# Expert weights loaded in pieces during attention, one key tile less on VectorE: a pre-LN attention and MLP kernel on one Trainium2 core

## The chip, the cores and the metric

The kernel runs on one core of a Trainium2 chip. A core has five engines with a queue of their own each, which keep only to the order of their own queue: TensorE (PE in the profile, its weight loads PEld), VectorE (DVE), ScalarE (ACT), GpSimd (POOL) and SyncE (SP, which here issues nearly all transfers). They wait for each other by semaphores. The metric is the device time of the whole program in microseconds.

## The reference

Attention with one shared key and value head, then an MLP for the eight best-scored rows, both behind a layer norm. S = 2048 rows, D = 448, 16 heads of 28, F = 1792.

```python
x = A_x
h = x + _A_ref(_layernorm(x), A_wq, A_wk, A_wv, A_wo)
    # q: 16 heads of 28; k, v: one head; softmax(q k^T * 28**-0.5) v, heads joined, @ wo
h2 = h + _B_ref(_layernorm(h), B_w_r, B_w_gate, B_w_up, B_w_down)
    # x: the normed rows; r = x @ w_r; the 8 rows with the largest r:
    # y = ((silu(x_sel @ w_gate) * (x_sel @ w_up)) @ w_down) * sigmoid(r_sel)
    # result: x, with y added to its 8 rows
```

## The kernel before, in words

**Blocks and key tiles.** The queries are cut into 16 blocks of 128 rows, the keys into 16 tiles of 128. One key tile of one block is four *strips* of scores, 128 keys by 512 columns (four heads by 128 queries), each made by one matmul `ps<-Q,K` (L815). A tile goes one of two ways.

- **ACT tile** (`act_tile`, `spill`): two strips at a time lie in two PSUM banks, and one ScalarE instruction takes the exponential of both (`P<-ps`, L870, 128x1024). A tile is two of these *units*. Four matmuls `ps<-P,Vs` (L845) add its product with V to the block's sum in bank 7.
- **DVE tile** (`dve_tile`): VectorE clips each strip into a 16-bit integer whose bits, read as bf16, are a rough exponential (`Y<-ps`, L891, four per tile). GpSimd adds two constants to a copy of the tile (`Yc<-Y`, L902, two per tile), and TensorE multiplies all three versions with three scaled copies of V: twelve matmuls of L845 where an ACT tile has four.

`_ND` gives for each block how many of its 16 tiles go the DVE way: 87 of 256 before. V has a column of ones, so the block's sum also holds the softmax denominators.

**The head.** x arrives in six loads. For each of seven groups of tiles (0; 1; 2 and 3; 4 and 5; 6 and 7; 8 to 11; 12 to 15) `group` computes the statistics, normalizes (`of`, L738), transposes on TensorE (L749), copies out (`xnT`, L754) and projects K (L621, `ps<-xnT,wk_rep`) and V. VectorE writes K's first copy (L764). The second copy, for the other two strips of a tile, is made by two DMAs `K<-K` on SP's queue, and the scores of the tile wait for them. `q_project` makes Q of a block. `weights` issues the output projection `wo` in four DMAs, each of which waits for the one before it, and the MLP's gate and up weights: `wg_sb` and `wu_sb`, each one DMA of 1344 KB and one of 224 KB.

**Between blocks.** When a block's products are done, `evict` copies bank 7 (`Ot`, L929). The denominators then go out to DRAM and back in another layout (`l_scr<-Ot`, `Lall<-l_scr`), VectorE takes reciprocals (`Rc`, L935), and these go out and come back broadcast (`l_scr<-Rc`, `Rb<-l_scr`). `On` (L938) multiplies them in. `out_proj` adds x and multiplies with `wo`, and VectorE and ScalarE make the row's second norm (`of`, L988), which is stored in `n_rows` and in the output. All these transfers stand in SP's queue, in order, and an instruction that waits there holds up those behind it.

**The end.** `stage1` loads the down weights in one DMA of 1568 KB (`wd_sb`, which lies over `xnT`) and preselects eight rows out of each of the first 14 blocks: their addresses go out (`cidx<-gidx`) and GpSimd gathers them (`wqx<-n_rows,cidx`, L1066). `tail` finishes the last block, selects the best eight rows and runs the MLP on them.

**What sets the order.** The functions record operations with a duration, reads and writes. `_Flow.plan` then lays them out once, at build time, from those durations and a table of weights (`_W`, `_WIN`, `_LOOK`, `_LATE`, `_HOLD`) and fixes each engine's order. Nothing is reordered on the chip. Bank 7 holds the running sum; the other seven banks are handed out by the plan.

Of the kernel before, what the change touches and what calls it, by code (L numbers as in the profile page):

```python
# [506 lines left out]
def _fast(nc, G, sb, ps, psb, flag, scr, rows, A_x, A_wq, A_wk, A_wv, A_wo, B_w_r, B_w_gate, B_w_up, B_w_down, out):  # L507
    S, D, H = A_x.shape[1], A_x.shape[2], 16
    DH = D // H
    FF = B_w_gate.shape[1]  # L510
# [416 lines left out]
    def evict(b):  # L927
# [10 lines left out]
        G.op(DV, lambda e: e.tensor_tensor(On[:, rb, :, :].rearrange("p h n -> p (h n)"), Ot[:, rb, :], Rb[:, rb, :],  # L938
                                           ALU.mult), 599, reads=[("Ot", rb), ("Rb", rb)], writes=[("On", rb)], lock=True)

# [860 lines left out]
```

## Time and profile before

| | before |
|---|---|
| median of 3 runs | 364.43 us (364.39 to 366.26) |
| the profiled execution | 365.21 us, span 363.2 us |
| ScalarE busy | 327.8 us (90%), 407 instructions |
| TensorE matmuls busy | 327.5 us (90%) |
| VectorE busy | 318.0 us (88%), 663 instructions |
| GpSimd busy | 194.3 us (54%) |
| mean granted TensorE clock | 0.968 |
| DMA traffic | 16.36 MB, mean 45 GB/s |

Busy shares are averages over stages. Three stages have different limits: the head (to about 45 us), in which keys are made and ScalarE often has no scores to work on, the long middle, and the tail after the last exponential. In the timeline a row gives start, duration, engine and line, operation, tile and count; idle time before it and what ended it stand in brackets. "SPq" rows are the issuing of a DMA, not its transfer.

### The profile page before, as it was taken

The page shows a single profiled execution, that of the slowest core. Times are in us where ns is not written, and L with a number is a line of the kernel's source. Part 1 is how long each engine was busy: PE and PEld are TensorE (multiplying, and loading weights), DVE is VectorE, ACT ScalarE, POOL GpSimd, SP SyncE. Part 2 cuts the span into 40 slices and gives each one's busy share as a digit, 9 for nine tenths or more (in the row PEclk, how much of TensorE's full clock was granted, in tenths as well). Part 3 has the DMA queues.
Part 4 walks back from the last instruction along what each step waited for, and adds up shares of the span by engine and source line. Part 5 has one row for each costly group of instructions (what it writes and reads, how often), then busy time and mean ns, then how long its engine had stood idle before and what let it go on. Part 6 is the DMA issues. An engine that isn't in the chain of part 4 may idle for free.

```text
span 363.2 us, 8869 instructions
## 1 busy us (share of the span) xinstructions
PE 327.5 (90%) x3690; PEld 109.8 (30%) x3690; DVE 318.0 (88%) x663; ACT 327.8 (90%) x407; POOL 194.3 (54%) x206
## 2 busy tenths in 40 slices
PE   3955989999999999999999999999999999999984
PEld 2623323232323222223232222323232322222344
DVE  7854669998989989999998999999988999999783
ACT  5543799999999999999999999999999999999950
POOL 8010027874656565866564656658563758675501
PEclk9976899999999999999999999999999999999995
DMA  7563000001001100101010101010011240010110
GB/s 181 130 230 137 10 7 3 15 20 28 32 19 41 31 27 29 32 5 56 4 47 14 55 3 43 19 30 29 29 33 31 81 153 32 13 47 8 56 35 9
DMA packets 18551, 16.36 MB, mean 45 GB/s; under 512 B 6558, under 2 KB 15614, under 8 KB 18506
## 3 DMA queue, kind: packets, MB, share of 16 engines
q1 hardware_dynamic: 17002, 15.18, 13.7%
q8 instruction: 30, 0.49, 0.6%
q10 hardware_dynamic: 1392, 0.45, 0.6%
q14 instruction: 15, 0.12, 0.1%
q0 software_dynamic: 112, 0.12, 0.1%
HBM read 11.78 MB, written 3.71 MB: 43 GB/s over the span
## 4 chain that ended last, share of the span: by engine, by line
ACT 77%; PE 10%; DMA 6%; DVE 4%; issue 1%; POOL 0%; POOLq 0%; ACTq 0%; SPq 0%; DVEq 0%
ACT P L870 75%; PE ps L621 5%; PE ps L815 3%; DMA K<-K 2%; DMA Rb<-l_scr 1%; PE ps L845 1%; DMA wqx<-in_A_wq_dram 1%; PE ps L749 1%; DMA l_scr<-Rc 1%; DVE Y L891 1%; DVE of L738 1%; ACT st L968 1%; DVE K L764 1%; ACT st L970 0%; ACT wqx L703 0%
## 5 line engine op out<-in xcount | busy, mean ns | idle before, releaser
L870 ACT ACTIVATE P<-ps 128x1024 bf16<-128x1024 f32 x338 | 314.4, 1209 | 13.6 <-PE ps L815 13.5
L902 POOL INT64_ADD Yc<-Y x174 | 182.2, 1059 | 139.3 <-DVE Y L891 126.0
L891 DVE TENSOR_SCALAR Y<-ps 128x512 int16<-128x512 f32 x348 | 220.3, 681 | 15.5 <-PE ps L815 15.0
L815 PE MATMUL ps<-Q,K 32*128 32x512 bf16 (+1 forms) x1024 | 151.0, 389 | 19.3 <-ACT P L870 10.0
L815 PEld LDWEIGHTS ps<-Q,K 32*128 32x128 bf16 (+1 forms) x1024 | 38.8, 91 | 148.0 <-ACT P L870 112.7
L845 PE MATMUL ps<-Yc,Vs 128*32 128x512 bf16 x696 | 62.3, 384 | 0.0
L845 PE MATMUL ps<-P,Vs 128*32 128x512 bf16 x676 | 60.8, 392 | 1.1 <-DVE Ot L929 0.9
L845 PE MATMUL ps<-Y,Vs 128*32 128x512 bf16 x348 | 34.2, 384 | 0.0
L845 PEld LDWEIGHTS ps<-P,Vs 128*32 128x32 bf16 x676 | 14.8, 94 | 31.0 <-issue 25.5
L621 PE MATMUL ps<-xnT,wqx 112*128 112x128 bf16 x256 | 21.7, 232 | 0.1
L845 PEld LDWEIGHTS ps<-Yc,Vs 128*32 128x32 bf16 x696 | 15.1, 94 | 20.1 <-issue 14.3
L621 PE MATMUL ps<-wo_pad,On 128*32 128x448 bf16 (+1 forms) x244 | 19.2, 357 | 0.0
L621 PEld LDWEIGHTS ps<-xnT,wqx 112*128 112x128 bf16 x256 | 16.0, 104 | 7.4 <-issue 4.8
L749 PE MATMUL ps<-ident,of 128*112 128x128 bf16 x64 | 6.9, 271 | 6.6 <-DVE of L729 5.5
L798 DVE TENSOR_SCALAR Q<-ps,qone 128x512 bf16<-128x512 f32 (+1 forms) x16 | 11.6, 727 | 1.0 <-PE ps L621 1.0
L845 PEld LDWEIGHTS ps<-Y,Vs 128*32 128x32 bf16 x348 | 9.1, 94 | 9.9 <-issue 9.1
L621 PE MATMUL ps<-x_sb,ident 128*32 128x448 bf16 (+1 forms) x82 | 10.4, 360 | 1.5 <-DVE Y L891 1.4
L966 DVE BATCH_NORM_STATS2 bn<-ps 128x6 f32<-128x448 f32 x15 | 9.4, 627 | 2.6 <-PE ps L621 2.6
L938 DVE TENSOR_TENSOR On<-Ot,Rb 128x512 bf16<-128x512 f32 x15 | 10.5, 701 | 0.7 <-DMA Rb<-l_scr 0.7
L764 DVE TENSOR_SCALAR K<-ps,kcol 128x128 bf16<-128x128 f32 (+2 forms) x8 | 4.4, 550 | 7.5 <-PE ps L621 7.4
L754 DVE COPY xnT<-ps 112x1024 bf16<-112x1024 bf16 (+1 forms) x9 | 5.6, 629 | 5.5 <-PE ps L749 5.3
L988 DVE TENSOR_SCALAR of<-ps,st 128x448 bf16<-128x448 f32 x14 | 10.3, 733 | 0.0
(159 smaller groups left out, 156.4 us busy)
## 6 DMA issues: line engine op xcount, KB each, us to landing
Rb<-l_scr SPq DMA_DIRECT2D x15, 256.0 KB
out_dram<-of SPq DMA_DIRECT2D x16, 112.0 KB, 2.1
n_rows<-of SPq DMA_DIRECT2D x14, 113.0 KB, 2.0
xnT<-in_B_w_down_dram SPq DMA_DIRECT2D x1, 1568.0 KB, 7.3
x_sb<-in_A_x_dram SPq DMA_DIRECT2D x3, 448.0 KB, 3.9
wg_sb<-in_B_w_gate_dram SPq DMA_DIRECT2D x1, 1344.0 KB, 8.4
wu_sb<-in_B_w_up_dram SPq DMA_DIRECT2D x1, 1344.0 KB, 6.4
wqx<-in_A_wq_dram ACTq DMA_DIRECT2D x1, 392.0 KB, 4.8
```

Of the source, the lines that this page charges most:

```text
L621: return lambda e: e.matmul(o() if callable(o) else o, lhsT=l, rhs=r, start=start, stop=stop)
L749: return lambda e: e.transpose(psb[0:CK, u.b[0], (ch * m + k) * 128:(ch * m + k + 1) * 128], of[:, a + k, ch * CK + cut(a, ch):(ch + 1) * ...
L764: G.op(DV, lambda e, r=r: e.tensor_scalar(K[:, r, sl], ps[:, uk.b[0], 0:w], kcol[:, r:r + 1], kcol[:, 2 + r:3 + r], ALU.mult, ALU.add), 19 ...
L798: G.op(DV, lambda e, c=c, src=src: e.tensor_scalar(Q[:, b % 3, c[0]:c[1], :], src(), qone[:, 0:1], None, ALU.add), 60 + n * 150, reads=[u. ...
L815: return e.matmul(ps[:, u.b[0] + q, :], lhsT=K[a:a + w, i % 2, j * 128:(j + 1) * 128], rhs=Q[a:a + w, b % 3, :, :].rearrange("p h n -> p ( ...
L845: return e.matmul(ps[32 * i:32 * i + 32, ACC, :], lhsT=Vs[:, v, j, :], rhs=src(i), start=info["first"] == o.idx, stop=info["last"] == o.idx)
L870: G.op(AC, lambda e, u=u, p=p, n=n: e.activation(P[:, p:p + n, :], ps[:, u.b[0]:u.b[0] + n, :], ACT.Exp, bias=EB, scale=OCT), 50.0 + 426.5 ...
L891: G.op(DV, lambda e, u=u, g0=g0: e.tensor_scalar(Y0[:, g0, :].bitcast(I16), ps[:, u.b[0], :], 0.0, TOP - STEP[-1], ALU.max, ALU.min), 599, ...
L902: G.op(PO, lambda e: e.int64_add(Yc[:, c, :, :].rearrange("p a b -> p (a b)").bitcast(I64), Y0[:, 4 * s:4 * s + 4, :].rearrange("p a b -> ...
L938: G.op(DV, lambda e: e.tensor_tensor(On[:, rb, :, :].rearrange("p h n -> p (h n)"), Ot[:, rb, :], Rb[:, rb, :], ALU.mult), 599, reads=[("O ...
L966: G.op(DV, lambda e: e.bn_stats(bn6[:, t, :], hp()), 545, reads=[u.key], writes=[("bn6", t)], free=u)
L988: G.op(DV, lambda e: e.tensor_scalar(of[:, t, 0:D], hp(), st[:, t, 2:3], st[:, t, 3:4], ALU.mult, ALU.add), 652, reads=[u.key, ("st2", t), ...
```

## The change

The gate and up weights leave `weights`. `evict` of block b now calls `load_mlp`: after `On` of block b, for b = 2 to 9, one piece is loaded, gate for even b and up for odd b: three chunks of 128 rows (448 KB) and one of 64 rows (224 KB) of each. `load_down` loads the down weights in four pieces, two after `On` of block 13 and two after that of block 14; each writes the keys of `xnT`, so each waits for the one before it. The tail's matmuls wait for all pieces. `_ND` has 86 tiles for VectorE instead of 87, in another distribution over the blocks, and the plan's weights are other numbers.

```diff
@@ the plan's table (a part)
-_ND = (3, 7, 4, 6, 7, 6, 5, 5, 6, 6, 6, 3, 7, 7, 4, 5)
+_ND = (3, 6, 5, 5, 7, 4, 7, 4, 5, 8, 6, 4, 6, 7, 4, 5)
-_LOOK = 123.4
+_LOOK = 317.5
@@ group, q_project: the plan's figures
-                    reads=["K1"] + [("K", 0, t) for t in tl_], lat=2100.0)
+                    reads=["K1"] + [("K", 0, t) for t in tl_], lat=2600.0)
-                             ...] for ch in range(NCH)], 470 if b == 0 else 235,
+                             ...] for ch in range(NCH)], 470 if b == 0 else 430 if b == 1 else 235,
@@ evict
-        G.op(DV, lambda e: e.tensor_tensor(On[:, rb, :, :].rearrange("p h n -> p (h n)"), Ot[:, rb, :], Rb[:, rb, :],
+        o = G.op(DV, lambda e: e.tensor_tensor(On[:, rb, :, :].rearrange("p h n -> p (h n)"), Ot[:, rb, :], Rb[:, rb, :],
                                            ALU.mult), 599, reads=[("Ot", rb), ("Rb", rb)], writes=[("On", rb)], lock=True)
+        load_mlp(b, [o])
+        if b >= NT - 3:
+            load_down(b - NT + 3, [o])
@@ weights
-        big = [xd[-1]]
-        for w_, A_, nm in ((wg_sb, B_w_gate, "wg"), (wu_sb, B_w_up, "wu")):
-            big.append(dma(w_[:, 0:3, :], A_[0:384].rearrange("(k p) n -> p k n", p=128), [nm], after=big[-1:]))
-            dma(w_[64:128, 3, :], A_[384:448], [nm + "3"], after=big[-1:])
@@ new functions
+    def load_mlp(b, after):
+        G.prio = b + 1.5
+        w_, A_, nm = ((wg_sb, B_w_gate, "wg"), (wu_sb, B_w_up, "wu"))[b % 2]
+        k = b // 2 - 1
+        if 0 <= k < 3:
+            dma(w_[:, k, :], A_[128 * k:128 * k + 128], [(nm, k)], after=after, lat=3500.0)
+        elif k == 3:
+            dma(w_[64:128, 3, :], A_[384:448], [(nm, 3)], after=after, lat=3500.0)
+
+    def load_down(h, after):
+        G.prio = NT - 1.9 + h
+        for k in (2 * h, 2 * h + 1):
+            c = slice((NFC + 3) // 4 * k, min((NFC + 3) // 4 * (k + 1), NFC))
+            dma(wd_sb[:, c, :], B_w_down.rearrange("(k p) n -> p k n", p=128)[:, c, :], [("wd", k)] + [("xnT", t) for t in range(NT)],
+                after=after, lat=3500.0)
@@ stage1
-        dma(wd_sb[:, :, :], B_w_down.rearrange("(k p) n -> p k n", p=128), ["wd_sb"] + [("xnT", k) for k in range(NT)])
```

**Place 1, SyncE's queue in the head.** Before, from the load of `w_rb` to the copies of K for tiles 6 and 7. The `K<-K` rows of 32x256 are, in order, tiles 2 and 3, tiles 4 and 5, tiles 6 and 7:

```order
L633 DMA w_rb<-in_B_w_r_dram 128x448
L633 DMA wg_sb<-in_B_w_gate_dram 128x3x1792
L633 DMA K<-K 32x256 x2
L633 DMA wo_pad<-in_A_wo_dram 28x4x448
L633 DMA wg_sb<-in_B_w_gate_dram 64x1792
L633 DMA wu_sb<-in_B_w_up_dram 128x3x1792
L633 DMA wo_pad<-in_A_wo_dram 28x4x448
L633 DMA wu_sb<-in_B_w_up_dram 64x1792
L633 DMA K<-K 32x256 x2
L633 DMA wo_pad<-in_A_wo_dram 28x4x448
L633 DMA K<-K 32x256 x2
```

The same stretch of SyncE's queue now:

```order
L633 DMA w_rb<-in_B_w_r_dram 128x448
L633 DMA K<-K 32x256 x2
L633 DMA wo_pad<-in_A_wo_dram 28x4x448 x3
L633 DMA K<-K 32x256 x4
L633 DMA K<-K 32x512 x4
```

The four weight loads are gone from the head, and the last three loads of `wo` now stand together, ahead of the copies for tiles 4 and 5.

**Place 2, TensorE's queue in the head.** Before, from the projection of K for tiles 6 and 7 (the first row) to the projection for tiles 8 to 11. `L749` are transposes, `L815` scores (four matmuls are one key tile), `L845` the products with V:

```order
L621 MATMUL ps<-xnT,wk_rep 128x256 x4
L621 MATMUL ps<-wv_sb,xnT 128x28 x8
L845 MATMUL ps<-P,Vs 32x512 x8
L815 MATMUL ps<-Q,K 128x512 x4
L749 MATMUL ps<-ident,of 112x128 x16
L815 MATMUL ps<-Q,K 128x512 x4
L845 MATMUL ps<-P,Vs 32x512 x4
L621 MATMUL ps<-xnT,wk_rep 128x512 x4
```

The same stretch of TensorE's queue now:

```order
L621 MATMUL ps<-xnT,wk_rep 128x256 x4
L621 MATMUL ps<-wv_sb,xnT 128x28 x8
L845 MATMUL ps<-P,Vs 32x512 x8
L749 MATMUL ps<-ident,of 112x128 x8
L815 MATMUL ps<-Q,K 128x512 x4
L749 MATMUL ps<-ident,of 112x128 x8
L815 MATMUL ps<-Q,K 128x512 x2
L621 MATMUL ps<-xnT,wk_rep 128x512 x4
```

Eight of the transposes for tiles 8 to 11 now stand ahead of the scores of tile 4 (the first `L815` row), the other eight behind them, and half a tile of scores moved behind the projection.

**Place 3, SyncE's queue between blocks.** Now, from the end of block 3 on; a bracket names the engine or the earlier DMA whose semaphore the issue waits for:

```order
L633 DMA l_scr<-Ot 4x512 [waits m_dve]
L633 DMA wg_sb<-in_B_w_gate_dram 128x1792 [waits m_dve]
L633 DMA Lall<-l_scr 128x16 [waits md42]
L633 DMA l_scr<-Rc 128x16 [waits m_dve]
L633 DMA n_rows<-of 128x452 [waits m_dve]
L633 DMA out_dram<-of 128x448
L633 DMA Rb<-l_scr 128x1x512 [waits md45]
L633 DMA wu_sb<-in_B_w_up_dram 128x1792 [waits m_dve]
```

Before, the same four transfers of a block's denominators, without a weight load among them:

```order
L633 DMA l_scr<-Ot 4x512 [waits m_dve]
L633 DMA Lall<-l_scr 128x16 [waits md40]
L633 DMA l_scr<-Rc 128x16 [waits m_dve]
L633 DMA Rb<-l_scr 128x1x512 [waits md42]
L633 DMA n_rows<-of 128x452 [waits m_dve]
L633 DMA out_dram<-of 128x448
```

In block 3 a gate piece (which waits for `On` of block 2) entered between the two transfers of the denominators, and the two stores of a finished block moved ahead of the broadcast. Blocks 5, 7 and 14 have a piece in the same place (in block 14 two pieces of the down weights). In the other blocks the piece stands behind the broadcast.

More of the change, by code (lines that the diff above doesn't have):

```diff
@@ L245 @@
     0, 0, 0, 0, 0, 0, 0, 0, 0, 0, 0, 0, 0, 0, 0, 0, 0, 0, 0, 0, 0, 0, 0, 0, 0, 0, 0, 0, 0, 0, 0, 0, 0, 0, 0, 0, 0, 0,
-    0, 0, 0, 0, 0, 0, 0, 0, 0, 0, 0, 0, 0)
+    0, 0, 0, 0, 0, 0, 0, 0, 0, 0, 0, 0)
 _ADD = 950.0
@@ L250 @@
 _NC = 6
-_ND = (3, 7, 4, 6, 7, 6, 5, 5, 6, 6, 6, 3, 7, 7, 4, 5)
-_W = {'A': -88.463, 'D': 4.412, 'C': 3.265, 'S': 39.182, 'P': 18.037, 'V': -39.83, 'G': -27.658, 'Q': -93.722, 'O':
-    -27.742, 'K': 23.522, 'E': 22.275, 'F': 14.519, 'L': 43.021}
+_ND = (3, 6, 5, 5, 7, 4, 7, 4, 5, 8, 6, 4, 6, 7, 4, 5)
+_W = {'A': -83.346, 'D': 50.973, 'C': -12.322, 'S': 65.974, 'P': 4.994, 'V': -21.541, 'G': -31.55, 'Q': -110.537, 'O':
+    -21.151, 'K': 42.072, 'E': 30.251, 'F': -3.107, 'L': 50.316}
 _SHIFT = 1060
-_LOOK = 123.4
-_WIN = {PE: 16.5, AC: 41.1, DV: 8.1, PO: 32.2, SP: 1.0}
-_LATE = (4, 105.9)
+_LOOK = 317.5
+_WIN = {PE: 8.1, AC: 4.9, DV: 7.9, PO: 101.0, SP: 1.0}
+_LATE = (4, 103.0)
 _MOST = {"A": 1, "D": 2, "M": 3, "T": 9}
 _TUNE = {}
-_HOLD = {'A': 3.4, 'D': 206.5}
+_HOLD = {'A': 2.0, 'D': 216.1}
 _LOW = 0
@@ L789, in q_project @@
                 G.op(PE, [mm(bank(u, c=slice((h - c[0]) * 128, (h - c[0] + 1) * 128)), wq_pad[0:CK, ch, h, :],
-                             xnT[0:CK, ch, b * 128:(b + 1) * 128], ch == 0, ch == NCH - 1) for ch in range(NCH)], 470 if b == 0 else 235,
+                             xnT[0:CK, ch, b * 128:(b + 1) * 128], ch == 0, ch == NCH - 1) for ch in range(NCH)], 470 if b == 0 else 430 if b == 1 else 235,
                      reads=[("wqp", ch) for ch in range(NCH)] + ["wq_pad", ("xnT", b)], writes=[u.key],
@@ L1167, in tail @@
                              xsel[:, c, :], c == 0, c == 3) for fc in range(HC) for c in range(4)], 850,
-                     reads=[nm, nm + "0", nm + "3", "xsel"], writes=[uh[k].key], take=uh[k])
+                     reads=[(nm, c) for c in range(4)] + [nm + "0", "xsel"], writes=[uh[k].key], take=uh[k])
         G.op(AC, lambda e: e.activation(sig[:, 0:8], ps[:, ut.b[0], 8:16], ACT.Exp, scale=-1.0), 200, reads=[ut.key],
@@ L1187, in tail @@
                          guT[:, HC * k + fc, :], fc == 0, fc == HC - 1) for c in range(4) for fc in range(HC)], 850,
-                 reads=[("guT", k), "wd_sb"], writes=[ud[k].key], take=ud[k])
+                 reads=[("guT", k)] + [("wd", c) for c in range(4)], writes=[ud[k].key], take=ud[k])
         G.op(DV, lambda e: e.tensor_copy(y0[:, :], ps[:, ud[0].b[0], 0:32]), 110, reads=[ud[0].key], writes=["y0"], free=ud[0])
```

## The prediction

> **What bounds the kernel now.** I read the groups first, then the windows by stage, then ScalarE's waits, then its timeline in the head and the queue of the engine that it waits for.
>
> ```profile
> L870 ACT ACTIVATE P<-ps 128x1024 bf16<-128x1024 f32 x338 | 314.4, 1209 | 13.6 <-PE ps L815 13.5
> L891 DVE TENSOR_SCALAR Y<-ps 128x512 int16<-128x512 f32 x348 | 220.3, 681 | 15.5 <-PE ps L815 15.0
> ```
>
> The dearest group is ScalarE's exponential. Three engines are busy for 88 to 90% of the span, so the totals don't say which one binds. The windows do (after the length: PE, PEld, DVE, ACT, POOL busy, with counts, clock, DMA share, GB/s):
>
> ```profile
> ...
> 11.10:45.48 34.38, 25.41 (x214) 13.64 (x214) 21.41 (x57) 17.70 (x26) 1.62 (x2) 0.80 0.38 120
> 45.48:343.90 298.42, 284.86 (x3206) 84.28 (x3206) 276.26 (x520) 298.06 (x349) 182.91 (x175) 1.00 0.11 32
> ...
> ```
>
> From 45.48 to 343.90 us ScalarE is idle for 0.36 us of 298.42: it is the bound there, and nothing that only relieves TensorE or VectorE can shorten this stage. From 11.10 to 45.48 it works 17.70 us of 34.38, so **16.7 us are lost in the head**. These are the places (in brackets the idle time ahead):
>
> ```profile
> 24.18 1.94 ACT L870 ACTIVATE P<-ps 128x1024 bf16<-128x1024 f32 x2 [4.81 <-PE ps L815]
> ...
> 34.46 1.94 ACT L870 ACTIVATE P<-ps 128x1024 bf16<-128x1024 f32 x2 [5.91 <-PE ps L815]
> ...
> 37.31 1.02 ACT L870 ACTIVATE P<-ps 128x1024 bf16<-128x1024 f32 x1 [0.92 <-PE ps L815]
> ```
>
> TensorE, in turn, waits for a transfer before both long gaps, the copies of K:
>
> ```profile
> 23.54 1.03 PE L815 MATMUL ps<-Q,K 64*128 64x512 bf16 x4 [3.71 <-DMA K<-K]
> ...
> 33.81 1.03 PE L815 MATMUL ps<-Q,K 64*128 64x512 bf16 x4 [4.28 <-DMA K<-K]
> ```
>
> SyncE's queue shows what these copies stand behind:
>
> ```profile
> 14.60 0.76 SPq L633 DMA_DIRECT2D wg_sb<-in_B_w_gate_dram  x1
> 16.49 1.15 SPq L633 DMA_DIRECT2D K<-K  x2
> 17.69 0.57 SPq L633 DMA_DIRECT2D wo_pad<-in_A_wo_dram  x1
> ...
> 23.64 0.59 SPq L633 DMA_DIRECT2D wu_sb<-in_B_w_up_dram  x1
> ...
> 30.07 0.49 SPq L633 DMA_DIRECT2D wu_sb<-in_B_w_up_dram  x1
> 30.61 1.23 SPq L633 DMA_DIRECT2D K<-K  x2
> ```
>
> **The change part by part.**
>
> *First gap: bytes.* The copies for tiles 2 and 3 are issued 1.9 us after 1344 KB of gate weights:
>
> ```profile
> 17.05 6.35 DMA K<-K
> wg_sb<-in_B_w_gate_dram SPq DMA_DIRECT2D x1, 1344.0 KB, 8.4
> K<-K SPq DMA_DIRECT2D x4, 32.0 KB, 2.0
> ```
>
> The chain gives the second copy 6.35 us, to 23.40; the larger copies later, with nothing beside them, take 2.0. Without the weights it lands at about 17.05 + 2.2 = 19.3. TensorE's queue now projects K after 12 instead of 16 matmuls of Q, which brings K forward by 0.4. So the unit at 24.18 comes at 19.5 to 19.8: 4.5 us earlier.
>
> *Second gap: the queue.* K for tiles 4 and 5 was ready long before its copy was issued:
>
> ```profile
> 25.58 0.54 DVE L764 TENSOR_SCALAR K<-ps,kcol 128x256 bf16<-128x256 f32 x1 [4.01 <-PE ps L621]
> 29.68 1.30 DVE L738 TENSOR_SCALAR of<-x_sb,mv,rstd 128x448 bf16<-128x448 bf16 x4
> ```
>
> Ready at 26.12, issued at 30.61, because SyncE stood at the small `wu_sb` load until the large one had landed (30.07). That wait goes; **next late** is one of two others. First, three `wo` loads now stand ahead of these copies, each waiting for the one before. None shows its landing; the nearest loads are a 112 KB piece of x and, with the gate weights beside it, `w_rb`:
>
> ```profile
> x_sb<-in_A_x_dram SPq DMA_DIRECT2D x2, 112.0 KB, 2.6
> w_rb<-in_B_w_r_dram SPq DMA_DIRECT2D x1, 112.0 KB, 3.7
> ```
>
> The first is issued at 17.2; at 2.6 each the third is out at 17.2 + 2 x 2.6 + 0.6 = 23.0, at 3.7 each at 25.2. I take 2.6, the nearer in conditions. K is ready at about 21.8 (4.3 earlier, behind the first gap), so the copies are issued at 23.0 and 23.6 and land at 25.7. Second, TensorE now has eight transposes ahead of these scores (place 2), for which VectorE must normalize tiles 8 and 9. That took place at 29.68; before it stand only K and statistics that also come 4.3 to 4.8 earlier, so it begins at about 25 and the transposes end at 26.3. The scores run at 26.3, the unit starts at 26.7, against 34.46: **7.8 us earlier**. If `wo` takes 3.7, the copies land at 28.0 and the gain is 6.1.
>
> *Small gaps.* The 0.92 at 37.31 and smaller ones behind it come from TensorE's slow projections; half a tile of scores moved behind one of them. I keep them, with 0.2 us of gain. **Head: -8.0 us**, between -6 and -10 (the upper end closes nearly all of these gaps).
>
> *One tile more on ScalarE.* Two more units. In the middle their pitch, from the chain, is 35.85 / 39 = 0.92 us:
>
> ```profile
> 45.48 35.85 ACT P L870 x39
> ```
>
> **+1.84 us**, since ScalarE has no idle time there. VectorE loses four strips (681 ns each, 2.4 to 2.7 us), GpSimd two additions, TensorE eight matmuls. That would be the gain if one of these bound; with ScalarE idle for 0.36 us it is worth nothing.
>
> *Pieces in the middle.* 2688 KB of gate and up weights cross in eight pieces. As bytes they are hidden: ScalarE was fully busy while the down weights crossed.
>
> ```profile
> 291.00:293.00 2.00, 1.79 (x15) 0.54 (x15) 2.00 (x5) 2.00 (x5) 0.55 (x1) 1.00 1.10 357
> xnT<-in_B_w_down_dram SPq DMA_DIRECT2D x1, 1568.0 KB, 7.3
> Lall<-l_scr SPq DMA_DIRECT2D x15, 8.0 KB, 1.7
> ...
> 63.20 0.36 SPq L633 DMA_DIRECT2D Lall<-l_scr  x1
> ...
> 67.47 0.24 DVE L935 RECIPROCAL Rc<-Lall 128x16 f32<-128x16 f32 x1
> ```
>
> The cost can only be a wait. A piece waits for `On`, and behind it on SyncE stand the transfers of the next block's denominators; for those wait `Rc` and `On` on VectorE, and for VectorE's banks TensorE. In blocks 3, 5 and 7 the piece is between `l_scr<-Ot` and `Lall` (place 3): 448 KB at 357 GB/s add 1.3 us to a transfer of 1.7. Before, `Rc` of block 0 began at 67.47; its `Lall`, issued at 63.20, was there at 64.9: 2.6 us of slack, out of which 1.3 (in block 7 about 2.8, since its `On` is later) must come. A short wait has a price in the trace, in block 6:
>
> ```profile
> 184.01 3.31 DMA l_scr<-Rc
> 187.34 5.30 DMA Rb<-l_scr
> DVE On L938 <- DMA Rb<-l_scr: 0.7, 1, 0.7
> ACT P L870 <- PE ps L815: 0.3, 1, 0.3
> ```
>
> VectorE waited 0.7 us for the broadcast, and ScalarE lost 0.3 us there, its only wait between 46 and 344 us. Block 3 also has the two stores of a finished block ahead of its broadcast. Nothing excludes four waits of 1.5 us, at 0.4 us lost per us: 2.5. I take **+0.5**, range 0 to 2.5.
>
> *The down weights.* In block 14 two pieces stand among the denominators' transfers, and two more are issued behind `cidx<-gidx`, while GpSimd gathers:
>
> ```profile
> 343.18 1.14 POOL L1066 DMA_INDIRECT wqx<-n_rows,cidx  x1 [0.93 <-DMA cidx<-gidx]
> wqx<-n_rows,cidx POOLq DMA_INDIRECT x1, 2.8
> 346.08 0.28 ACT L1076 ACTIVATE cst<-wqx,ebias 112x1 f32<-112x1 f32 x1
> ...
> 352.80 1.57 PE L621 MATMUL ps<-xsel,wg_sb 128*128 128x8 bf16 x56
> ```
>
> The gather lands at 346.0 and ScalarE needs it at 346.08: no slack, and the last block's scaling stands behind it. A 392 KB piece takes 1.1 us at 357 GB/s; it mostly passes before the gather's bytes start. The first matmuls with these weights come at 352.80, long after. [...] I take **+0.5**, range 0 to 2.
>
> *Sum* against the profiled execution: 365.21 - 8.0 + 1.84 + 0.5 + 0.5 = 360.05. That execution lies 0.78 above the median of the runs, 364.43; so the forecast for the median is 364.43 - 5.2 = **359.2 us**.
>
> **The clock.** A window gives TensorE's granted clock (0.67, before the DMA share) between the two gaps, and the timeline one kind of work behind the second gap and later:
>
> ```profile
> 24.18:34.46 10.28, 6.00 (x46) 2.42 (x44) 5.19 (x16) 4.15 (x6) 0.00 (x0) 0.67 0.62 204
> ...
> 38.18 1.77 PE L621 MATMUL ps<-xnT,wk_rep 112*128 112x512 bf16 x4
> ...
> 44.07 1.04 PE L621 MATMUL ps<-xnT,wk_rep 112*128 112x512 bf16 x4
> ```
>
> After the idles of 3.71 and 4.28 us the clock is low, and a projection takes 1.77 instead of 1.04 us. If the idles shrink, as forecast, to under 3 us, the clock may stay up, worth about 0.7 us at each of two projections on the path: 1.5 us more. The Trainium skill (TensorE: Matmul & The Clock Gate, "The HAM clock gate") gives about 3.4 us of idleness as the window after which the clock is halved; the trace agrees, and by that rule the faster case below is the likely one.
>
> **The rivals.**
>
> - *The clock stays up*: -1.5 more, 357.7. For it: both falls follow idles above 3.7. Against: the gaps of TensorE may add up in one window, and the transposes wait for VectorE, not for TensorE. Chance 0.2.
> - *The `wo` chain takes the place of the weights*: 3.7 us per load, head -6.0, waits of 1.5 beyond ScalarE's two units in place of 1.0: 364.43 - 6.0 + 1.84 + 1.5 = 361.8. For it: the loads are in series on SyncE. Against: no large load beside them. Chance 0.17.
> - *The pieces hold up the blocks, slower than before*: twelve weight loads where there were five. If each of the eight pieces makes VectorE wait so long that ScalarE loses 1 us, that is 8 us; with 1.5 in the tail, 364.43 - 8.0 + 1.84 + 9.5 = 367.8. It decides from 0.7 us per piece on. For it: a load of 224 KB took 3.2 us where one of 1344 KB took 8.4, so a piece costs more than its bytes.
>
> ```profile
> wu_sb<-in_B_w_up_dram SPq DMA_DIRECT2D x1, 224.0 KB, 3.2
> ```
>
>   Against: four of the eight stand behind the broadcast, with 7 us until the next block's transfers, and 0.7 us of waiting cost only 0.3. Chance 0.06. The Trainium skill (DMA: Bandwidth & Descriptors, "Rules for kernel authors") asks for at least 1 MiB per DMA, against this change; it gives about 2.0 us of fixed cost per DMA ("Anatomy of one DMA"), an estimate of 14 us for seven more, if none were hidden.
> - *The new order starves ScalarE in the middle*: 1% of idle time there is 3 us, 362.2 to 364. The order is new throughout; for it nothing in the profile, against it four strips less and 5% of idle time on TensorE. Chance 0.1.
> - *The change doesn't do what it says*: the queue shows that it does; 0.
>
> **How the numbers follow.** Forecast 0.47, 358.5 to 361. With the faster case below and the two milder ones above it, the range is 356.5 to 363.0; its upper end lies within the starved case, its lower end at a head of -10 with half its other costs. Half a percent, about what a measurement of this kernel can tell from no change, is 1.8 us. Faster by more (under 362.6): 0.47 + 0.2 + 0.14 = 0.81; within: 0.12; slower: 0.07.
>
> **What would show it.** Right: no weights on the queue before 60 us; the `K<-K` steps of the chain near 2 us; the unit after the second gap starts near 27, and ScalarE is continuous from about 37; the middle has 340 units at 0.92 with under 1 us of idle time. Wrong: `wo_pad` as releaser of SyncE at 23 to 28 us with the copies behind it; ScalarE waits at blocks 3, 5, 7 or 14, with `Rb<-l_scr` or `Lall` ahead of VectorE; a second stretch where ScalarE's share falls below 99%.

## The result, and the profile after

| | before | after |
|---|---|---|
| median, in one comparison of 19 runs each | 365.64 us | 361.98 us (358.66 to 365.01) |
| the profiled execution, and its span | 365.21, 363.2 us | 361.09, 359.3 us |
| ratio of the runs, 95% interval | | 0.9895 [0.9869, 0.9920] |

The change takes off 3.7 us, 1.05%. The forecast was 5.2 us. The groups of the changed kernel (columns as before):

```profile
L870 ACT ACTIVATE P<-ps 128x1024 bf16<-128x1024 f32 x340 | 316.8, 1199 | 8.2 <-PE ps L815 7.8
...
L891 DVE TENSOR_SCALAR Y<-ps 128x512 int16<-128x512 f32 x344 | 217.1, 682 | 20.0 <-PE ps L815 19.5
...
L938 DVE TENSOR_TENSOR On<-Ot,Rb 128x512 bf16<-128x512 f32 x15 | 11.3, 755 | 2.7 <-DMA Rb<-l_scr 2.6
```

ScalarE's idle time ahead of the exponential fell from 13.6 to 8.2 us, by less than the head alone should have saved. VectorE now waits 2.6 us for the broadcast of the denominators, where it waited 0.7. The windows show the two stages apart (columns as in the prediction: after the length the five engines' busy time, then clock, DMA share, GB/s):

```profile
11.10:37.00 25.90, 21.21 (x219) 12.30 (x218) 20.95 (x57) 18.83 (x27) 1.62 (x2) 1.00 0.13 33
37.00:340.20 303.20, 284.25 (x3196) 83.78 (x3194) 274.51 (x516) 299.59 (x350) 179.40 (x173) 0.99 0.13 41
```

The last exponential ends at 340.20 us. In the head the clock stays at 1.00 and ScalarE does more work in 25.90 us than it did in 34.38. In the middle it is idle for 3.61 us, where it was idle for 0.36. (The expectations below say 3.9; that window ended 0.3 us later, in the tail.) ScalarE's timeline shows both:

```profile
19.87 2.85 ACT L870 ACTIVATE P<-ps 128x1024 bf16<-128x1024 f32 x3 [1.03 <-PE ps L815]
...
25.95 1.02 ACT L870 ACTIVATE P<-ps 128x1024 bf16<-128x1024 f32 x1 [2.05 <-PE ps L815]
...
36.81 37.69 ACT L870 ACTIVATE P<-ps 128x1024 bf16<-128x1024 f32 x41 [0.23 <-PE ps L815]
...
124.81 2.15 ACT L870 ACTIVATE P<-ps 128x1024 bf16<-128x1024 f32 x2 [1.00 <-PE ps L815]
127.41 1.02 ACT L870 ACTIVATE P<-ps 128x1024 bf16<-128x1024 f32 x1 [0.44 <-PE ps L815]
128.91 1.02 ACT L870 ACTIVATE P<-ps 128x1024 bf16<-128x1024 f32 x1 [0.30 <-PE ps L815]
...
165.94 3.77 ACT L870 ACTIVATE P<-ps 128x1024 bf16<-128x1024 f32 x4 [0.62 <-PE ps L815]
```

The unit that stood at 24.18 behind the first gap begins at 19.87 and the one at 34.46 at 25.95. From 36.81 on ScalarE is continuous, with 18 units done; before, it had done 17 at 45.48. At 0.92 us a unit the head has gained 45.48 - 36.81 + 0.92 = 9.6 us. The middle loses part of it again, near 125 (block 3), 166 (block 5) and 284 us (block 11), and 0.57 us at 339 us. In block 3 the queue of SyncE shows what stands ahead of the broadcast:

```profile
113.19 0.32 SPq L633 DMA_DIRECT2D l_scr<-Rc  x1
115.92 0.32 SPq L633 DMA_DIRECT2D n_rows<-of  x1
116.28 0.43 SPq L633 DMA_DIRECT2D out_dram<-of  x1
116.76 0.55 SPq L633 DMA_DIRECT2D Rb<-l_scr  x1
```

The broadcast `Rb` could go once `l_scr<-Rc` has landed. But the two stores of a finished block stand ahead of it, and they wait for their row until 115.92. VectorE then stands 1.82 us at `On`, at 120.7 to 122.5 us, and ScalarE's gaps follow 2 us later. Stores ahead of the broadcast are not enough by themselves: in the kernel before they stand ahead of `l_scr<-Rc` and `Rb` in block 3 too, but there the row was ready when the reciprocals were (stores issued at 122.84 and 123.20, `Rb` at 125.54), and ScalarE lost nothing.

### The profile page after: what moved, and what is told of

It reads as the page before. It is cut to its first block, busy times and chain, and to the rows that moved or that the text cites. A ratio compares the mean times of both kernels' runs of the same rounds, so it can differ in the third digit from the quotient of the medians.

```text
span 359.3 us, 8864 instructions
## 1 busy us (share of the span) xinstructions
PE 322.6 (90%) x3682; PEld 108.0 (30%) x3682; DVE 316.1 (88%) x659; ACT 330.6 (92%) x409; POOL 191.2 (53%) x204
## 4 chain that ended last, share of the span: by engine, by line
ACT 60%; DVE 15%; PE 12%; DMA 9%; issue 2%; SPq 1%; ACTq 0%; POOL 0%; POOLq 0%; DVEq 0%
ACT P L870 58%; DVE Y L891 5%; PE ps L621 5%; DMA Rb<-l_scr 4%; PE ps L815 4%; PE ps L845 3%; DMA n_rows<-of 1%; DMA Lall<-l_scr 1%; DVE On L938 1%; DMA K<-K 1%; DVE bn L716 1%; SPq L633 1%; DVE of L738 1%; DVE junk L979 1%; DMA wqx<-n_rows,cidx 1%
## 5 line engine op out<-in xcount | busy, mean ns | idle before, releaser
L902 POOL INT64_ADD Yc<-Y x172 | 179.1, 1053 | 138.6 <-DVE Y L891 128.7
L891 DVE TENSOR_SCALAR Y<-ps 128x512 int16<-128x512 f32 x344 | 217.1, 682 | 20.0 <-PE ps L815 19.5
L815 PE MATMUL ps<-Q,K 32*128 32x512 bf16 (+1 forms) x1024 | 149.2, 388 | 15.7 <-ACT P L870 12.2
L815 PEld LDWEIGHTS ps<-Q,K 32*128 32x128 bf16 (+1 forms) x1024 | 38.4, 91 | 143.7 <-ACT P L870 116.7
L845 PE MATMUL ps<-Yc,Vs 128*32 128x512 bf16 x688 | 63.9, 384 | 0.2
L845 PE MATMUL ps<-P,Vs 128*32 128x512 bf16 x680 | 61.1, 387 | 1.8 <-DVE Ot L929 1.2
L845 PE MATMUL ps<-Y,Vs 128*32 128x512 bf16 x344 | 34.1, 387 | 0.0
L845 PEld LDWEIGHTS ps<-P,Vs 128*32 128x32 bf16 x680 | 15.0, 94 | 33.0 <-issue 26.7
L845 PEld LDWEIGHTS ps<-Yc,Vs 128*32 128x32 bf16 x688 | 16.5, 95 | 19.5 <-issue 12.8
L938 DVE TENSOR_TENSOR On<-Ot,Rb 128x512 bf16<-128x512 f32 x15 | 11.3, 755 | 2.7 <-DMA Rb<-l_scr 2.6
L749 PE MATMUL ps<-ident,of 128*112 128x128 bf16 x64 | 6.1, 248 | 6.6 <-DVE of L729 5.5
L845 PEld LDWEIGHTS ps<-Y,Vs 128*32 128x32 bf16 x344 | 9.0, 95 | 10.1 <-issue 9.2
L991 DVE TENSOR_SCALAR of<-ps,st 128x448 bf16<-128x448 f32 x14 | 10.3, 737 | 0.1
L929 DVE COPY Ot<-ps 128x512 f32<-128x512 f32 x15 | 10.1, 676 | 0.0
L979 DVE SCALAR_TENSOR_TENSOR junk<-ps,st,w_rb 128x448 bf16<-128x448 f32 x15 | 10.1, 675 | 0.0
```

What stands on the lines that cost most here:

```text
L815: return e.matmul(ps[:, u.b[0] + q, :], lhsT=K[a:a + w, i % 2, j * 128:(j + 1) * 128], rhs=Q[a:a + w, b % 3, :, :].rearrange("p h n -> p ( ...
L845: return e.matmul(ps[32 * i:32 * i + 32, ACC, :], lhsT=Vs[:, v, j, :], rhs=src(i), start=info["first"] == o.idx, stop=info["last"] == o.idx)
L891: G.op(DV, lambda e, u=u, g0=g0: e.tensor_scalar(Y0[:, g0, :].bitcast(I16), ps[:, u.b[0], :], 0.0, TOP - STEP[-1], ALU.max, ALU.min), 599, ...
L902: G.op(PO, lambda e: e.int64_add(Yc[:, c, :, :].rearrange("p a b -> p (a b)").bitcast(I64), Y0[:, 4 * s:4 * s + 4, :].rearrange("p a b -> ...
L929: o = G.op(DV, lambda e: e.tensor_copy(Ot[:, rb, :], ps[:, ACC, :]), 598, reads=[pk(ACC)], writes=[("Ot", rb)], prio=b - 10.0, after=blk[b ...
L938: o = G.op(DV, lambda e: e.tensor_tensor(On[:, rb, :, :].rearrange("p h n -> p (h n)"), Ot[:, rb, :], Rb[:, rb, :], ALU.mult), 599, reads= ...
```

## The experiments

Two things were in dispute: what held the head (the bytes of the weights, or SyncE standing in its queue), and what costs the middle its idle time, **theory P**, the pieces of weights, or **theory S**, the new order of the work, above all the stores ahead of the broadcast. Replanning would change every engine's order at once. So nearly all experiments leave the plan as it is and move named transfers in SyncE's queue afterwards; the orders of TensorE, VectorE, ScalarE and GpSimd stay those of the kernel that is edited:

```diff
+def _planned(self, plan=_Flow.plan):
+    span = plan(self)
...
+    for what, behind in _MOVES:
+        o, p = at[what], at[behind]
+        for l in (self.orders[SP], self.seq):
+            l.remove(o)
+            l.insert(l.index(p) + 1, o)
+    return span
```

A transfer is named by what it writes and a count: `('K', 1, 12, 1)` is the last copy of K, `('scr1', 3)` the `l_scr<-Rc` and `('scr0', 3)` the `l_scr<-Ot` of block 3, `('Rb', 1)` with count 1 its broadcast.

| run | edit | us, median (runs) | ratio to before, 95% |
|---|---|---|---|
| h2 | before; large gate load behind K of tiles 2, 3 | 368.38 (1) | |
| h3 | before; waiting `wu` load behind all K | 363.18 (1) | |
| h1, h6 | before; all four loads behind all K | 355.08 (6), 354.42 (6) | 0.9725 [0.9690, 0.9760], 0.9700 [0.9644, 0.9756] |
| e1 | after; broadcast ahead of the stores, 3 blocks | 360.81 (6) | 0.9849 [0.9798, 0.9901] |
| e2 | after; three gate pieces behind the broadcast | 365.55 (10) | 0.9969 [0.9933, 1.0005] |
| t1 | after, planned with before's table | 361.04 (4) | 0.9873 [0.9833, 0.9912] |
| h4 | before; stores ahead of the broadcast, block 2 | 370.55 (1) | |
| e3 | after; eight pieces behind all K | 360.93 (5) | 0.9891 [0.9826, 0.9956] |
| e4 | e3 and e1 | 361.09 (6) | 0.9845 [0.9800, 0.9890] |
| t2 | before, planned with after's table | 370.61 (4) | 1.0128 [1.0082, 1.0173] |
| h5 | before's order; the pieces in the middle | 354.18 (6) | 0.9685 [0.9635, 0.9735] |

The kernel before took 365.3 to 365.9 us beside them.

### The head: h2, h3, h1

```diff
+_MOVES = [(('wg', 0), ("('K', 1, 2, 1)", 0))]
```

> The kernel before; only the large gate load (1344 KB) is moved behind the copies of K for tiles 2 and 3 on SyncE's queue. Theory B (the first gap is bytes beside the copy, as forecast): the first K<-K step takes about 2.2 us instead of 6.35, ScalarE's unit that began at 24.18 begins at 19.5 to 20.5, TensorE's first long idle falls under 3 us and the granted clock stays 1.00 there. The second gap stays, since SyncE still stands at the small wu load until the large one has landed, which is now 1 to 3 us later: the unit that began at 34.46 begins at 35 to 37, and the run is 0.5 to 2.5 us slower than before. Rival Q (the first gap is not bytes, but TensorE's own order or the transposes): the unit stays near 24.

The unit behind the first gap, and the next one, with the load of `wu` from the chain below it:

```profile
20.74 2.86 ACT L870 ACTIVATE P<-ps 128x1024 bf16<-128x1024 f32 x3 [0.81 <-PE ps L815]
...
37.43 1.94 ACT L870 ACTIVATE P<-ps 128x1024 bf16<-128x1024 f32 x2 [12.64 <-PE ps L815]
```

```profile
26.01 6.96 DMA wu_sb<-in_B_w_up_dram
```

The first gap goes from 4.81 to 0.81 us: it was bytes, as forecast. All the rest waits for K of tiles 4 and 5, whose copies stand behind the load that waits till 32.97. The second unit came 0.4 us later than expected, and this one run was 3.1 us slower, 0.6 beyond what was expected.

```diff
+_MOVES = [(('wu3', 0), ("('K', 1, 12, 1)", 0))]
```

> The kernel before; only the small wu load (224 KB), which waits for the large one, is moved behind the last copy of K on SyncE's queue, so that nothing stands ahead of the copies of K for tiles 4 and 5 but loads that are already issued; all bytes stay where they are. Theory B (the second gap is SyncE standing at that load): the copies are issued at 26.2 to 26.8 instead of 30.61, and the unit that began at 34.46 begins at 29.5 (a copy of 2.3 us) and the run is 4 to 5 us faster. Rival R (the bytes of the large wu load, in flight till about 30, hold the copies too): the copies land at 30 to 31, the unit begins at 31 to 32, and 2.5 to 3.5 us are gained. The first gap stays under both (24.2).

The copy in the chain, and the unit behind it:

```profile
26.66 4.45 DMA K<-K
```

```profile
31.68 2.85 ACT L870 ACTIVATE P<-ps 128x1024 bf16<-128x1024 f32 x3 [3.19 <-PE ps L815]
```

The copies were issued at 26.09 instead of 30.61, but took 4.45 us instead of 2.44 beside the large load. The unit came 2.8 us earlier: rival R. (This one run was 2.2 us faster than the median of before.) The second gap is the queue, and behind it bytes too.

```diff
+_MOVES = [(('wu3', 0), ("('K', 1, 12, 1)", 0)), (('wu', 0), ("('K', 1, 12, 1)", 0)), (('wg3', 0), ("('K', 1, 12, 1)", 0)), (('wg', 0), ("('K', 1, 12, 1)", 0))]
+_APART = ('wg', 'wg3', 'wu', 'wu3')
```

(`_APART` takes away the waits of these four for each other.)

> The kernel before with its four gate and up loads whole, but issued on SyncE behind the last copy of K, without waits among them; every other engine's order is that of before, and 87 tiles on VectorE. If the weights ahead of the copies of K are what costs the head: idle time of ScalarE from 11 us to its last long gap falls from 16.7 to 8 or 9 us, the copies of K take about 2 us, the middle stays without idle time (under 0.7 us), the span falls by 7 to 9 us to 354 to 356, ratio 0.977 to 0.981, that is faster than the changed kernel. If the head's gain came from the new order on TensorE and VectorE: 4 to 5 us at most, ratio 0.987 or more. If 3136 KB at once in the middle hold up block 0: a ScalarE gap of over 1 us between 45 and 60 us.

Before's order with a free head, and the middle in its windows:

```profile
11.10:34.30 23.20, 20.22 (x216) 11.50 (x214) 20.56 (x57) 17.52 (x25) 1.62 (x2) 1.00 0.15 39
34.30:333.88 299.58, 285.54 (x3206) 84.45 (x3204) 276.11 (x520) 298.33 (x349) 182.89 (x175) 0.99 0.14 43
```

ScalarE has 17 units done at 34.30 us, 11.2 us earlier than before. The run is 10.3 us faster than before, more than the 7 to 9 expected, and **6.9 us faster than the change**: the whole loads, at the right place in the queue, do more than the change as made. Up to the last exponential at 333.88 us ScalarE is idle for 1.25 us, 0.34 of them at 43 us, while the loads cross, and 0.79 in block 6, where before lost 0.3. In h6, the same kernel, its waits from 45 to 325 us are 0.2, so the bytes cost the middle little or nothing.

### The middle: e1, e2, t1, h4

```diff
+_MOVES = [(("('Rb', 1)", 1), ("('scr1', 3)", 0)), (("('Rb', 1)", 2), ("('scr1', 5)", 0)), (("('Rb', 1)", 5), ("('scr1', 11)", 0))]
```

> The changed kernel with one thing moved on SyncE's queue: in blocks 3, 5 and 11 the broadcast of the reciprocals (Rb) is issued ahead of the two stores of the finished block, not behind them; every other engine's order is the same. Theory S (the stores ahead of the broadcast make VectorE, and so ScalarE, wait in the middle): Rb is issued about 1.5 to 2.9 us after Rc in these blocks instead of 3.8 to 5.0, VectorE's waits for Rb at On (2.6 us in total) go to under 0.3 us, and ScalarE's idle time in the middle falls from 3.9 us to 1.0 to 1.5 us; the span falls by about 2.5 us to 356.8, the ratio to before to 0.982. Theory P (the weight pieces among the blocks' transfers cost it): unchanged within 0.5 us, since every piece is where it was.

The waits of ScalarE between 40 and 342 us, and of VectorE (total, times, longest):

```profile
ACT P L870 <- PE ps L815: 1.8, 3, 0.8
```

```profile
DVE On L938 <- DMA Rb<-l_scr: 0.7, 2, 0.4
```

VectorE's waits fall from 2.6 to 0.7 us and ScalarE's from 3.4 to 1.8; the gaps of blocks 3 and 11, 2.24 us together, are gone. That is less than theory S forecast. What is left is 0.62 in block 5, where moving the broadcast did not help, 0.82 at 338 us, and 0.39 at 49 us, where the clock had fallen (0.73 from 46 to 52 us). The median is only 1.2 us lower, and the intervals overlap.

```diff
+_MOVES = [(("('wg', 0)", 0), ("('Rb', 1)", 1)), (("('wg', 1)", 0), ("('Rb', 1)", 2)), (("('wg', 2)", 0), ("('Rb', 1)", 3))]
```

> The changed kernel with the gate pieces of 448 KB in blocks 3, 5 and 7 issued behind the broadcast Rb instead of ahead of Lall; every other engine's order is the same. Theory S: ScalarE's idle time in the middle stays between 3.2 and 4.2 us and the waits for Rb in blocks 3 and 5 stay above 0.5 us each, ratio to before 0.988 to 0.991. Theory P: the idle time falls by 2 us or more, ratio 0.983 or less.

SyncE's queue in block 3, and ScalarE behind it:

```profile
116.05 0.55 SPq L633 DMA_DIRECT2D Rb<-l_scr  x1
116.64 0.49 SPq L633 DMA_DIRECT2D wg_sb<-in_B_w_gate_dram  x1
```

```profile
125.25 1.02 ACT L870 ACTIVATE P<-ps 128x1024 bf16<-128x1024 f32 x1 [2.15 <-PE ps L815]
...
168.03 1.02 ACT L870 ACTIVATE P<-ps 128x1024 bf16<-128x1024 f32 x1 [1.73 <-PE ps L815]
```

This gave neither theory's number: 3.6 us slower than the change. 448 KB issued 0.6 us behind the broadcast travel beside it: `Rb` takes 6.31 and 6.03 us in blocks 3 and 5, where it took 5.76 and 5.25, and VectorE's waits for it rise from 2.6 to 4.5 us. So the pieces can cost at this place. Whether they cost where the change has them, ahead of `Lall`, this run can't say; e3 and h5 do.

```diff
-_ND = (3, 6, 5, 5, 7, 4, 7, 4, 5, 8, 6, 4, 6, 7, 4, 5)
+_ND = (3, 7, 4, 6, 7, 6, 5, 5, 6, 6, 6, 3, 7, 7, 4, 5)
...
```

(The whole table of before, with 87 tiles, in the changed kernel; the plan is made anew.)

> The changed kernel with the table of numbers of before (87 tiles on VectorE, the old weights of the plan): the loads in pieces alone. Head as in the changed kernel (ScalarE continuous from 36 to 38 us). Without the added tile 1.84 us less work on ScalarE. If pieces by themselves cost the middle under 0.5 us each place and the old table packs as before: span 353 to 356, ratio 0.976 to 0.981. If any plan with pieces loses what the changed kernel lost in the middle: ScalarE idle by 3 us or more there, ratio 0.983 to 0.986.

ScalarE's waits between 40 and 342 us:

```profile
ACT P L870 <- PE ps L815: 3.1, 5, 1.6
ACT Rb L1111 <- DVE Ot L1109: 2.1, 1, 2.1
ACT P L870 <- PE ps L845: 1.3, 2, 1.1
```

The head is that of the change (continuous from 36.58 us), and the middle loses as much at other places: 4.4 us of waits for scores and products, and 2.1 more behind the last exponential. So the new table is not needed for the head, and the old table does not help the middle once the plan is made with the pieces in it.

```diff
+_MOVES = [(("('Rb', 0)", 1), ("('out', 1)", 0))]
```

> The kernel before; in block 2 alone the broadcast Rb is moved behind the two stores of a finished block, n_rows and out, as it stands in block 3 of the changed kernel. Theory S (stores ahead of the broadcast are what costs in the middle): Rb is issued 3 to 4 us later than before, VectorE waits 1.0 to 2.5 us at On of block 2, and ScalarE, which has no idle time there before, loses 0.6 to 1.7 us between 110 and 125 us. Rival O (the plan's order with one tile more or less on VectorE matters, the broadcast has slack): VectorE waits under 0.5 and ScalarE loses under 0.2.

SyncE's queue in block 2, and VectorE and ScalarE behind it:

```profile
110.77 0.32 SPq L633 DMA_DIRECT2D n_rows<-of  x1
111.13 0.43 SPq L633 DMA_DIRECT2D out_dram<-of  x1
111.61 0.55 SPq L633 DMA_DIRECT2D Rb<-l_scr  x1
```

```profile
117.34 0.69 DVE L938 TENSOR_TENSOR On<-Ot,Rb 128x512 bf16<-128x512 f32 x1 [2.42 <-DMA Rb<-l_scr]
```

```profile
120.09 2.03 ACT L870 ACTIVATE P<-ps 128x1024 bf16<-128x1024 f32 x2 [1.51 <-PE ps L815]
122.56 1.02 ACT L870 ACTIVATE P<-ps 128x1024 bf16<-128x1024 f32 x1 [0.44 <-PE ps L815]
124.07 1.02 ACT L870 ACTIVATE P<-ps 128x1024 bf16<-128x1024 f32 x1 [0.31 <-PE ps L815]
```

The signature of block 3 of the change, in the kernel before, by one move: theory S. The broadcast went out 5.1 us behind `l_scr<-Rc`, which was issued at 106.50 us; before, it was 1.4. Of the 3.7 us between them `On` had slack for about 1.3 and waited 2.42. That also gives a price: 2.42 us of waiting for 1.51 + 0.44 + 0.31 = 2.26 us of ScalarE, **0.93 per us**; theory S had expected 0.6 to 1.7 us of ScalarE, and the prediction had taken 0.4 per us from a single wait of 0.7. (This one run was 5.2 us above the median of before. 1.5 of the rest were lost at 52 to 60 us, well ahead of the move, where the clock had fallen to 0.57, and 0.84 at 138 us; whether the move caused that one, and what remains, was not traced.)

### Pieces and order apart: e3, e4, h5

```diff
+_MOVES = [(("('wu', 3)", 0), ("('K', 1, 12, 1)", 0)),
...
+    (("('wg', 0)", 0), ("('K', 1, 12, 1)", 0))]
```

(All eight pieces, which then wait for nothing.)

> The changed kernel, with the order of all engines but SyncE kept; the eight pieces of the gate and up weights are issued behind the last copy of K (at about 36 us) and no longer wait for On. So the middle has the changed kernel's order without pieces. Theory P (pieces in the middle cost ScalarE's idle time there, 3.9 us): ScalarE's waits for scores in the middle fall to under 1 us and the time to 357.5 to 359 us (before at 365.5). Theory S (the order costs them: stores ahead of the broadcast in blocks 3, 5 and 11, whatever the pieces do): the waits at blocks 3, 5 and 11 stay within 0.5 us of 3.4 and the time stays at 361 to 362.5.

SyncE's queue in block 3, without the pieces, the waits of `On` in blocks 3, 5 and 11, and ScalarE's waits between 40 and 342 us:

```profile
116.80 0.54 SPq L633 DMA_DIRECT2D Rb<-l_scr  x1
```

```profile
122.30 0.69 DVE L938 TENSOR_TENSOR On<-Ot,Rb 128x512 bf16<-128x512 f32 x1 [1.54 <-DMA Rb<-l_scr]
...
162.80 1.28 DVE L938 TENSOR_TENSOR On<-Ot,Rb 128x512 bf16<-128x512 f32 x1 [1.41 <-DMA Rb<-l_scr]
...
281.63 0.84 DVE L938 TENSOR_TENSOR On<-Ot,Rb 128x512 bf16<-128x512 f32 x1 [0.84 <-DMA Rb<-l_scr]
```

```profile
ACT P L870 <- PE ps L815: 3.9, 5, 1.6
```

With no gate or up piece in the middle the broadcast goes out at the same time (116.80 against 116.76), ScalarE's gaps stay at the same three blocks (0.71, 1.63 and 0.48 us, where the change has 1.74, 0.62 and 0.50), and the time is the same. Theory P falls for these eight pieces. The three waits of `On`, 3.79 us together, cost ScalarE 2.82 here, 0.74 per us.

> The changed kernel with both edits: the eight pieces behind the last copy of K, and in blocks 3, 5 and 11 the broadcast ahead of the two stores. The order of all engines but SyncE is the changed kernel's. Theory S (the place of the broadcast costs the middle its 3.5 us, the pieces add little): ScalarE's waits for scores between 40 and 342 us fall from 3.9 to 0.5 to 1.5, and the time is 2 to 3 us under that of e3_pieces_early, 358 to 359 us with before at 365.3; what is left to h1_weights_late (355.1) is then the unit pair of the 86th tile (1.84) and 1 to 1.5 us of the head. Theory P+S (pieces and order each cost): the same here, but e1_broadcast_first would then have been slower than this by over 1.5 us. Rival N (the order of the other engines has too little slack, whatever SyncE does): waits of over 2.5 us stay, at other places, and the time stays above 360.

(The edit is those of e3 and e1 together.) ScalarE's waits between 40 and 342 us, VectorE's, and two windows (columns as above):

```profile
ACT P L870 <- PE ps L815: 4.1, 7, 0.9
```

```profile
DVE On L938 <- DMA Rb<-l_scr: 0.4, 1, 0.4
```

```profile
46.00:52.00 6.00, 6.00 (x40) 1.57 (x39) 4.09 (x8) 4.47 (x6) 4.38 (x5) 0.50 0.78 236
52.00:58.00 6.00, 6.00 (x54) 1.90 (x52) 4.63 (x8) 4.97 (x6) 2.20 (x3) 0.69 0.00 2
```

VectorE's wait is gone, as S says. But ScalarE's total and the median are rival N's. The windows show why: here the granted clock fell to 0.50 and 0.69, and 2.5 of the 4.1 us lie there; 1.6 are left. (The eight pieces still cross in the first window, 236 GB/s, but the clock fell there in e1 too, to 0.73, with 3 GB/s.) The runs differ in this. Of the six, the two with a mean clock of 0.98 or more took 357.54 and 358.36 us, the other four (0.965 to 0.970) 360.9 to 362.4. At 0.98 or more the change took 360.5 (median of 8), e3 360.7 (of 4), e1 357.4 and 358.6. Compared in this way, which was chosen after the fact, the place of the broadcast is worth 2 to 3 us and the pieces nothing. The medians alone don't show it.

```diff
-            big.append(dma(w_[:, 0:3, :], A_[0:384].rearrange("(k p) n -> p k n", p=128), [nm], after=big[-1:]))
+            big.append(dma(w_[:, 0, :], A_[0:128], [(nm, 0)], after=big[-1:]))
...
+_MOVES = [(("('wg', 0)", 0), ("('scr0', 3)", 0)), (("('wu', 0)", 0), ("('scr0', 4)", 0)),
...
+    (("('wg', 3)", 0), ("('scr0', 9)", 0)), (("('wu', 3)", 0), ("('scr0', 10)", 0))]
```

> The kernel before, with its order on TensorE, VectorE, ScalarE and GpSimd and its 87 tiles; the gate and up weights are loaded in the changed kernel's eight pieces, all eight between l_scr<-Ot and Lall of blocks 3 to 10 (the changed kernel has four of them there). The head has no weights. Theory S (pieces at this place are free; the changed kernel's loss in the middle is its order): the time is within 1 us of h1_weights_late of the same call, 354.5 to 356, and ScalarE's waits between 45 and 325 us stay under 1.5. Theory P (pieces ahead of Lall hold up the blocks): 0.5 us per piece, 358 to 360, with VectorE waiting for Lall or Rb in blocks 3 to 10.

> h1_weights_late once more, on the same chip as h5_pieces_middle: 354 to 356.5 under both theories.

SyncE's queue of h5 in block 3, and its waits between 45 and 325 us:

```profile
106.51 0.51 SPq L633 DMA_DIRECT2D l_scr<-Ot  x1
107.07 0.44 SPq L633 DMA_DIRECT2D wg_sb<-in_B_w_gate_dram  x1
108.21 0.32 SPq L633 DMA_DIRECT2D Lall<-l_scr  x1
```

```profile
DVE On L938 <- DMA Rb<-l_scr: 0.6, 1, 0.6
```

All eight pieces stand where the change has three of its gate pieces (blocks 3, 5 and 7; the expectation says four), and here they wait for nothing, while those of the change wait for an `On`. `Lall` takes 2.3 us in the median instead of 1.7, but VectorE waits no longer than with no piece (0.7 in h6). ScalarE's waits there are 1.8 us in this profile, of which 1.6 lie at 44 to 50 us, ahead of the first piece, with the clock at 0.63. 354.18 against 354.42 us: **the gate and up pieces are free**. This is theory S in its wide sense, the order of the work, and the fastest version. It has t1's tiles and gate and up pieces; t1 took 361.04. What differs is the order that the plan made, that t1's pieces wait, and t1's down weights in pieces.

No run moves the down pieces alone, so what they cost is not shown. In block 14 of the change one of them stands ahead of `Lall`, which then takes 3.79 us, and VectorE waits 0.3 us for it. ScalarE's gap at 339 us (0.57 us; 0.65 to 0.92 in e1, e3 and e4) may come from there; the tail behind the last exponential is no longer than before.

### The table alone: t2

The table of the change in the kernel before, with the loads in the head; the diff is that of `_ND` to `_HOLD` in the change.

> The kernel before with its weight loads, only the plan's table taken from the changed kernel (86 tiles for VectorE, other weights). Theory H (the gain is the head without weight loads; the table gains nothing): both head gaps stay, with the unit pair of one tile more on ScalarE (+1.84) and 0.5 to 3 us of new waits in the middle, where its queue too has stores ahead of the broadcast: 367 to 370 us with before at 365.3. Rival T (the table brings the gain: fewer strips on VectorE): 362 to 364.

ScalarE in the head:

```profile
24.01 1.94 ACT L870 ACTIVATE P<-ps 128x1024 bf16<-128x1024 f32 x2 [4.90 <-PE ps L815]
...
34.27 1.94 ACT L870 ACTIVATE P<-ps 128x1024 bf16<-128x1024 f32 x2 [5.19 <-PE ps L815]
```

Both gaps stay, and the run is 4.7 us slower than before, a little more than H's range. 1.9 us of that lie outside the profiled span (371.06 - 367.2 = 3.9 us, where before had 2.0); why was not tried.

## Why the prediction was right, and which terms were off

The direction and the range held; the point was 2.8 us too low against the medians, or 1.5 in terms of the gain. That it was no more is partly luck: the head gained 1.6 us more than forecast and the middle lost 2.75 more, and the two errors took each other off in part.

- **First gap, bytes: right.** Forecast 19.5 to 19.8, measured 19.87; h2 removes it by one move.
- **Second gap: right in place, half right in mechanism.** Forecast 26.7, measured 25.95. The prediction put it to SyncE's queue; h3 shows that the queue alone is worth 2.8 us and that bytes hold the copies as well. Since the change removes both, the number held. What is late next is what was forecast: the copies went out at 22.59 (forecast 23.0), and the transposes, which wait for VectorE's rows, came last.
- **Head, -8.0 forecast, -9.6 measured.** 0.75 us come from the second gap. The rest, 0.85, fits the clock: in the profiled execution it stayed at 1.00 and the first of the two projections took 1.04 us where it took 1.77 (the second took 1.04 before, too). That is the rival "the clock stays up" at about half its price of 1.5; it was not run by itself, and it is not so in every run (below): in e1, with TensorE's same order and a clock of 0.78, the stretch from the first gap's unit to the second's was 0.6 us longer (20.20 to 26.89 against 19.87 to 25.95).
- **One tile more, +1.84: held**, as far as the count goes (340 units instead of 338); it was not run by itself.
- **Pieces in the middle, +0.5 with 0 to 2.5: the step that failed.** The middle lost 3.61 - 0.36 = 3.25 us. The prediction looked for the cost in the pieces of the gate and up weights, and they cost nothing there (e3, h5). (Their bytes are 3136 KB, not 2688, and three stand ahead of `Lall` and five behind a broadcast, not four and four; neither figure enters the term.) It named the right thing in one clause, "Block 3 also has the two stores of a finished block ahead of its broadcast", and did not price it. And it gave the rival "the new order starves ScalarE in the middle" 0.1, with "for it nothing in the profile". What the runs showed in its place: the order that the plan made, with SyncE standing at stores that wait for their row while the broadcast is ready to go, costs 2.24 us in blocks 3 and 11 (e1); 0.62 in block 5 and 0.57 at 339 us are not explained by the place of the broadcast. Part of this could have been asked beforehand: the order listing shows in which blocks the stores stand ahead of `Rb`, and the trace shows how long `Rb` takes (5.30 us). They do not show when the row will be ready. The price of a wait was too low as well, 0.4 where h4 has 0.93 and e3 0.74.
- **Tail, +0.5: nothing.** From the last exponential to the end it was 363.2 - 343.9 = 19.3 us and is 359.3 - 340.2 = 19.1.
- **The rival of slower pieces.** Its estimate of 14 us, if none were hidden, uses a fixed cost per DMA that the Trainium skill (DMA: Bandwidth & Descriptors, "Anatomy of one DMA") gives for transfers issued by GpSimd, while SyncE issues these. The case did not come: all eight were hidden (h5).

The terms add up to -9.6 + 1.84 + 3.25 - 0.2 = -4.7 us, the spans differ by 3.9. The 0.8 between them lie in ScalarE's busy time: 299.78 us for 322 units from 36.81 on, 298.06 for 321 before, where one unit is 0.92; why was not traced. Set against the profiled execution of h1 (span 353.1 us), the change's is 6.2 us longer: 1.84 for the tile, 3.61 - 1.25 = 2.4 in the middle, 1.6 in the head (18 units done at 36.81 against 17 at 34.30), and the rest, 0.4, mostly ScalarE's busy time again. Which entries of the table make the order worse was not tried.

## What to carry to other kernels

When a load is moved and the schedule is made anew, these are two changes: hold the order fixed and move only the load, then see what the order is worth by itself (here the one gained 11 us and the other, with the added tile, gave back 8). An order with little slack should be read for what stands ahead of each transfer that an engine waits for, a store that waits for its data above all. In a stage whose bound is hardly ever idle, a wait of a nearly full engine beside it can cost most of its length (here 0.74 and 0.93 per us).
